# Loads of x four steps later, earlier second halves of W, filling products and earlier copies of R in a fused attention and channel-mix kernel

## The chip, the cores and the metric

The kernel runs on one core of a Trainium2 chip. The core has five engines that run their own instruction queues: TensorE (PE in the profile; its weight loads are PEld), VectorE (DVE), ScalarE (ACT), GpSimd (POOL) and SyncE (SP), which issues nearly all DMAs here. They wait for each other through semaphores. The metric is the device time of one execution in microseconds (us); the time before is 1131.95 us, the median of three runs (1128.4 to 1132.33).

## What is computed

Two layers follow one another. The first is an induced attention: 32 inducing vectors attend over the 12608 rows of x, and the rows of x then attend over the 32 results. The second is a channel mix of width 1024 with a gate, in which every row is mixed with the row before it.

```python
def _attn_ref(x, inducing):              # x: (4, 12608, 128), inducing: (32, 128)
    ...
    def mab(q, kv):
        s = scale * (q @ kv.transpose(0, 2, 1))
        s = s - s.max(-1, keepdims=True)
        a = np.exp(s)
        a /= a.sum(-1, keepdims=True) + 1e-09
        return a @ kv
    h = mab(I, x)
    return mab(x, h).astype(np.float32)

def _moe_ref(x, mu_k, mu_r, w_k, w_v, w_r):   # w_k: (128, 1024), w_v: (1024, 128), w_r: (128, 128)
    x_prev = np.concatenate([np.zeros((B, 1, D), dtype=np.float32), x[:, :-1, :]], axis=1)
    xk = mu_k * x + (1.0 - mu_k) * x_prev
    xr = mu_r * x + (1.0 - mu_r) * x_prev
    k = np.maximum(xk @ w_k, 0.0)
    v = k * k @ w_v
    r = 1.0 / (1.0 + np.exp(-(xr @ w_r)))
    return (r * v).astype(np.float32)
```

All is float32; the kernel splits several float32 matrices into a high part and a low rest (`kh` and `kl`, `ah` and `al`, `wvh` and `wvl`), whose products are added.

## The kernel before

Each of the four batches has 12608 rows: six blocks of 2048 rows and a tail of 320. A block has four groups of 512 rows, so a batch has 25 groups. A group is worked in four **units** of 256 of the 1024 channels, 100 units a batch, 400 in all. The main loop takes one unit in each **step**, and everything else is hung onto these steps by hand: `at(n, f)` runs `f` at the end of step n, `soon(n, f)` runs it in step n right after the unit's first products. Inside an engine the order of the program is the order of execution.

A step n does the following. `up` (L809 and L811) multiplies the attention weights `R` of the group, once as they stand and once shifted by one row, by `W[0]` and `W[1]`, which hold the two mixes of the attention result with w_k (512 columns in the first half, 512 in the second, and 128 for the gate); it writes one of two PSUM tiles `ps_a`. `square` then makes `k_t` on DVE (L821), `kh` on ACT (L826) or, for the steps listed in `high_vector`, on DVE (L823), and the full square on ACT (L827); POOL makes the rest `kl` (L829). `down` (L840, six products) works on the unit of four steps before (`LAG`). In every fourth step `zgate` (L798 and L799) makes the gate, `gate` (L845) and `store` (L856, then the DMAs of L864, one for two groups) the output.

For the next batch, `stage_a` runs beside these units, one block in twelve steps (a **segment**, starting at step s; six beside each of the first three batches, numbered 1 to 18 below): `load_x` (L193) brings a block of x, 1 MB, into one of three buffers `xb`; `btr(c)` for c = 0 to 3, at s-1, s, s+1 and s+3, transposes a quarter of it on DVE (L344) into one of four `xs`, and sends it by four DMAs (L347) to `xt`; `scores` at s+9 (L372, eight products in the profile) multiplies `xt` by the inducing vectors. At step s+1 `load_x` is called for the block that the next segment transposes from its own s-1, which is this segment's s+11. In the same segments `stage_b` turns the block's scores into weights: `low` writes the last of them (L660), and `spread` (L670, four DMAs a group, with the one-column copy `halo`, L593) brings them to `R`; the first of these DMAs that needs `low` waits for it at the head of SP's queue. So SP's queue holds, in the order of the program, the DMAs of `btr`, the loads of x, the spreads and the stores.

The first batch starts differently. `head()` does its first attention, and `start()` orders what stands between it and the first units: `wa` and `wb` are the first and the second halves of `W[0]` and `W[1]`, each as a product (L537), a high part on ACT (L540) and a low rest on DVE (L543); `wg` are the gate's columns. The first four groups of weights do not go by DMA: `place(k)` makes `hi` (ACT, L762), `lo` (DVE, L765) and `put` (transposes on PE, L771, and a copy to `R` on ACT, L773). `spin(n)` makes n products of the identity whose result nobody reads.

The lines that the change touches are L480 and L482 (the loads), L914 to L918 (`spin`), L1013 to L1034 (`start`) and L1037 (`high_vector`).

Of the kernel before, what the change touches and what calls it, by code (L numbers as in the profile page):

```python
# [8 lines left out]
F32 = mybir.dt.float32  # L9
# [10 lines left out]
def kernel(  # L20
# [15 lines left out]
    P = 128  # L36
    Q = 4
    FC = F // P
    G = 512
# [19 lines left out]
    pa = ctx.enter_context(tc.tile_pool(name="pa", bufs=2, space=bass.MemoryType.PSUM))  # L59
# [4 lines left out]
    def pb_tile(bank=None):  # L64

        return pb.tile([P, G], F32, name="pb_" + (bank or next(banks)))
# [92 lines left out]
    def groups(j):  # L159

        w = G if j < NBLK - 1 else TAIL // Q
        return [(j * BLK + i * w, w) for i in range(Q)]
# [16 lines left out]
    def load_x(b, j, pair=None, pieces=1):  # L179

        S = batches[b]
        gr = groups(j)
        w = gr[0][1]
        if w < G:
            t = xn_pool.tile([P, Q, C], F32, name="xl", bufs=1)
            nc.sync.dma_start(out=t[:w], in_=x[b, gr[0][0]:, :].rearrange("(i p) c -> p i c", p=w))
            for i in range(Q):
                S.xn[j, i] = t[:, i:i + 1, :]
            return
        src = x[b, j * BLK:(j + 1) * BLK, :].rearrange("(p s) c -> p s c", p=P)  # L190
        if b > 0:
            t = xn_pool.tile([P, Q * Q, C], F32, name="xb", bufs=3)
            nc.sync.dma_start(out=t, in_=src)  # L193
            S.xb[j] = t
            return
        if pair is not None:
            S.xh[j] = [next(pair).rearrange("p u (k c) -> p (u k) c", c=C) for _ in range(2)]
        else:
            t = xn_pool.tile([P, Q * Q, C], F32, name="xb", bufs=3)
            S.xh[j] = [t[:, :2 * Q, :], t[:, 2 * Q:, :]]  # L200
        n = 2 * Q // pieces
        for h in range(2):
            for o in range(0, 2 * Q, n):
                nc.sync.dma_start(out=S.xh[j][h][:, o:o + n, :], in_=src[:, 2 * Q * h + o:2 * Q * h + o + n, :])
# [121 lines left out]
    def stage_a(b, j, at, t):  # L326
# [8 lines left out]
        jt = NBLK - 1  # L335
# [141 lines left out]
        k = order_a.index((b, j))  # L477
        for bn, jn in order_a[k + 1:]:
            if jn < NBLK - 1:
                at(t + 1, lambda: load_x(bn, jn))  # L480
                if jn == NBLK - 2:
                    at(t + 1, lambda: load_x(bn, jt))  # L482
                break


# [102 lines left out]
    def halo(S, g, far=True):  # L588

        if g == 0:  # L590
            nc.vector.memset(S.R[g].bitcast(F32)[:, 0:1], 0.0)
        elif far:
            nc.sync.dma_start(out=S.R[g].bitcast(F32)[:, 0:1], in_=S.R[g - 1].bitcast(F32)[:, G:G + 1])  # L593
        else:
            nc.vector.tensor_copy(out=S.R[g][:, 0:1], in_=S.R[g - 1].bitcast(F32)[:, G:G + 1])
# [272 lines left out]
    def run(th):  # L868
        for f in th:
            f()  # L870
# [40 lines left out]
    ab = [stage_a_head(j, k, hs) for k, (j, hs) in enumerate(order_h)]  # L911
    weights, hfin, gates, wpart = combine(0)

    def spin(n):  # L914

        ps = pa.tile([P, 2, G], F32, name="ps_a")
        for i in range(n):
            nc.tensor.matmul(out=ps[:, 0, :P], lhsT=ident, rhs=ident, start=True, stop=True)  # L918


    def head():
# [37 lines left out]
        u.sums()  # L959
        v.expo()  # L960
        spin(3)
        w.scores()
        for h in range(2):
# [5 lines left out]
        for c in range(FC // cg):  # L969
            split_wv(c)  # L970
        spin(5)
        v.etrans()
        v.sums()
        v.hmm(0)
        w.etrans()
        w.sums()
        v.acc()
        spin(1)
        weights()
        w.hmm(1)  # L980
# [8 lines left out]
    def at(n, f):  # L989
        events.setdefault(n, []).append(f)  # L990

    def soon(n, f):
        early.setdefault(n, []).append(f)

    def start():

        part0, pl0 = stage_b_head([0, 1])
        part1, pl1 = stage_b_head([2, 3])
        sc0, tu0, df0, ex0, nm0 = part0([0])
        sc1, tu1, df1, ex1, nm1 = part0([1])  # L1000
        sc2, tu2, df2, ex2, nm2 = part1([0, 1])
        (hi0, lo0, put0), (hi1, lo1, put1) = pl0
        box = {}

        def bank():
            return pv.tile([P, G], F32, name="ps_v")

        def gate_bank(s):
            if s == 0:
                box["g"] = bank()  # L1010
            return box["g"][:, s * C:(s + 1) * C]

        wa = [wpart(s, 0, bank) for s in range(2)]  # L1013
        wb = [wpart(s, 1, bank) for s in range(2)]
        wg = [wpart(s, None, lambda s=s: gate_bank(s)) for s in range(2)]
        assert F // G == 2
        S = batches[0]
        run([gates, sc0, sc1, tu0, df0, ex0, wa[0][0], wa[1][0], tu1, nm0, wa[0][1], hi0, wa[1][1], lo0, wa[0][2], put0,
             df1, ex1, wa[1][2], nm1, hi1, lambda: halo(S, 1, far=False)])
        for n, f in ((0, wb[0][0]), (0, wb[0][1]), (1, wb[1][0]), (1, wb[1][1]), (1, put1)):  # L1020
            soon(n, f)
        for n, f in ((0, lo1), (0, wb[0][2]), (1, wb[1][2]), (1, sc2), (2, tu2), (2, df2), (2, ex2), (3, nm2)):
            at(n, f)
        for prod, high, low in wg:
            at(1, prod)
        for prod, high, low in wg:
            at(1, high)
            at(2, low)
        for k, (high, low, put) in enumerate(pl1):
            at(3, high)  # L1030
            at(4, low)
            at(2 * k + 6, put)
            at(4 * k + 4, lambda k=k: halo(S, k + 2, far=False))
        soon(4, lambda: units[0][0].zgate(first=True))  # L1034

    SEG = 12
    high_vector = {3}  # L1037
    for b in range(B):
        t = b * UB + (4 if b == 0 else 0)
        for j in range(NBLK - 1):  # L1040
            s = t + SEG * j
            high_vector |= {s + 4, s + 8}
            if b + 1 < B:
                stage_a(b + 1, j, at, s)
            first = b == 0 and j == 0
            stage_b(b, j + 1, at, s + 1 + first, first)
        if b + 1 < B:
            s = t + SEG * (NBLK - 1)
            combine(b + 1, at, s)
            stage_b(b + 1, 0, at, s + 13, b == 0)  # L1050
# [6 lines left out]
    with tc.manual_schedule():  # L1057
        head()
        start()
        for n in range(len(units) + LAG + 2):  # L1060
            grp, u = units[n] if n < len(units) else (None, n % NU)
            old, ou = units[n - LAG] if LAG <= n < len(units) + LAG else (None, 0)
            m = n - LAG - 1
            if 0 <= m < len(units) and units[m][1] == NU - 1:
                units[m][0].gate()
            if grp is not None:
                grp.up(u)
                run(early.pop(n, []))
                if n >= NU and u == 1:
                    grp.zgate()  # L1070
                low = grp.square(u, n in high_vector)
                low(nc.vector if n == end else nc.gpsimd, 0, grp.w)
            if 1 <= m <= len(units) and units[m - 1][1] == NU - 1:
                units[m - 1][0].store()
            if old is not None:
                old.down(ou)
            run(events.pop(n, []))
# [30 lines left out]
```

## Time and profile before

| what | before |
|---|---|
| median of three runs | 1131.95 us (1128.4 to 1132.33) |
| profiled execution, time | 1130.93 us |
| profiled execution, span | 1128.7 us |
| PE busy | 1098.4 us (97%) |
| ACT, POOL, DVE busy | 969.8, 952.9, 912.0 us |
| PE busy from 0 to 44 us | 35.14 of 44 us |
| PE busy from 44 to 75 us | 24.74 of 31 us |
| PE busy from 75 to 320 us | 243.92 of 245 us |
| PE busy from 320 to 600 us | 274.81 of 280 us |
| PE busy from 600 to 850 us | 247.63 of 250 us |
| PE busy from 850 us to the end | 272.19 of 278.7 us |

The profile is of one execution on the chip. Matmuls overlap in the records (each of the up products is listed with 0.40 us, and the next starts 0.23 us later), and their ends are modelled, so a wait of PE shows as a gap or as a group of products that takes longer than its equals. In the rows of the order of time, the columns are the start and the length in us, the engine (SPq is SP's queue at the issue of a DMA), the line, the operation, what is written and read, and the count; brackets give the idle time before and what ended it. The granted clock of PE is a column of its own in the table of windows (PEclk).

### The profile page before, as it was taken

How to read it: one execution, taken by the hardware profiler on the slowest of the kernel's cores; microseconds unless marked ns; L12 is line 12 of the kernel's file. 1: busy time of each engine (PE TensorE's matmuls, PEld its weight loads, DVE VectorE, ACT ScalarE, POOL GpSimd, SP SyncE). 2: the span in 40 equal slices, each digit the busy share in tenths (PEclk: the TensorE clock that was granted, in tenths of full speed). 3: DMA queues.
4: the chain of work that ended last, by engine and by line, in shares of the span. 5: the costliest groups of instructions: out<-in, count | busy, mean ns of one | idle time of the engine just before them, and what ended most of it. 6: DMA issues, size and time to landing. Idle time of an engine off the chain costs nothing.

```text
span 1128.7 us, 17615 instructions
## 1 busy us (share of the span) xinstructions
PE 1098.4 (97%) x5699; PEld 834.1 (74%) x5699; DVE 912.0 (81%) x1318; ACT 969.8 (86%) x1096; POOL 952.9 (84%) x417
## 2 busy tenths in 40 slices
PE   7889999999999999999999999999999999999997
PEld 5567777777776777777777777777778777777886
DVE  6798889887787999887777889898777888887665
ACT  6588888888888888887998889888889999989996
POOL 2279888888897888898888988888888899999997
PEclk9999999999999999999999999999999999999999
DMA  9024555642334655554144554654223233242212
GB/s 344 4 77 89 112 126 119 139 122 36 60 75 109 133 124 117 118 103 104 23 81 88 111 123 113 134 133 82 50 52 62 44 63 61 56 76 57 44 29 34
DMA packets 264458, 102.30 MB, mean 91 GB/s; under 512 B 234256, under 2 KB 237488, under 8 KB 262064
## 3 DMA queue, kind: packets, MB, share of 16 engines
q1 hardware_dynamic: 263360, 101.10, 41.0%
q8 instruction: 45, 0.74, 0.3%
q14 instruction: 45, 0.37, 0.1%
q10 hardware_dynamic: 1008, 0.10, 0.1%
HBM read 28.07 MB, written 25.82 MB: 48 GB/s over the span
## 4 chain that ended last, share of the span: by engine, by line
PE 78%; DVE 9%; ACT 5%; DMA 3%; issue 3%; SPq 1%; POOL 1%; DVEq 0%; ACTq 0%; POOLq 0%
PE ps_v L840 39%; PE ps_a L809 15%; PE ps_a L811 14%; DVE k_t L821 3%; PE pb_a L372 2%; PE pb_b L616 2%; ACT kh L826 2%; PE ps_v L798 2%; PE ps_v L799 2%; DMA xt<-xs 2%; PE pb_a L441 1%; ACT k_t L827 1%; SPq L347 1%; DMA xb<-in_x_dram 1%; POOL kl L829 1%
## 5 line engine op out<-in xcount | busy, mean ns | idle before, releaser
L829 POOL TENSOR_TENSOR kl<-k_t,kh 128x1024 fp32r<-128x1024 f32 (+1 forms) x399 | 938.5, 2385 | 140.7 <-ACT k_t L827 106.7
L821 DVE TENSOR_SCALAR k_t<-ps_a 128x1024 f32<-128x1024 f32 (+1 forms) x400 | 479.6, 1199 | 146.8 <-PE ps_a L811 123.2
L827 ACT ACTIVATE k_t<-k_t 128x1024 f32<-128x1024 f32 (+1 forms) x400 | 418.4, 1048 | 37.6 <-DVE kh L823 25.6
L826 ACT ACTIVATE kh<-k_t 128x1024 fp32r<-128x1024 f32 (+1 forms) x351 | 364.8, 1039 | 85.2 <-PE ps_v L840 49.5
L809 PE MATMUL ps_a<-R,W 128*128 128x512 f32 (+1 forms) x800 | 324.6, 406 | 4.1 <-ACT R L773 2.8
L811 PE MATMUL ps_a<-R,W 128*128 128x512 f32 (+1 forms) x800 | 314.6, 393 | 0.2 <-DVE W L543 0.2
L840 PE MATMUL ps_v<-kh,wvh 128*128 128x512 f32 (+1 forms) x800 | 247.8, 391 | 0.0
L840 PE MATMUL ps_v<-kl,wvh 128*128 128x512 f32 (+1 forms) x800 | 246.7, 390 | 0.7
L840 PE MATMUL ps_v<-kh,wvl 128*128 128x512 f32 (+1 forms) x800 | 247.0, 390 | 0.0
L809 PEld LDWEIGHTS ps_a<-R,W 128*128 128x128 f32 x800 | 151.2, 189 | 78.0 <-issue 14.4
L840 PEld LDWEIGHTS ps_v<-kl,wvh 128*128 128x128 f32 x800 | 148.5, 188 | 37.6 <-POOL kl L829 5.3
L840 PEld LDWEIGHTS ps_v<-kh,wvh 128*128 128x128 f32 x800 | 149.5, 188 | 34.7
L840 PEld LDWEIGHTS ps_v<-kh,wvl 128*128 128x128 f32 x800 | 149.5, 188 | 33.8
L811 PEld LDWEIGHTS ps_a<-R,W 128*128 128x128 f32 x800 | 150.9, 189 | 31.4 <-DVE W L543 0.8
L845 DVE TENSOR_TENSOR oT<-ps_v,rT 128x512 f32<-128x512 f32 (+1 forms) x100 | 66.6, 666 | 1.8
L856 DVE STREAM_TRANSPOSE ot<-oT 128x512 f32<-128x512 f32 x96 | 67.1, 699 | 0.0
L823 DVE SCALAR_TENSOR_TENSOR kh<-ps_a,k_t 128x1024 fp32r<-128x1024 f32 x49 | 60.0, 1224 | 5.1
L801 ACT ACTIVATE rT<-ps_v 128x512 f32<-128x512 f32 (+1 forms) x99 | 57.8, 584 | 0.3
L344 DVE STREAM_TRANSPOSE xs<-xb 128x512 f32<-128x512 f32 x72 | 49.9, 693 | 0.2
L801 ACT ACT_TABLE_LOAD x31 | 39.8, 1283 | 0.6
L798 PE MATMUL ps_v<-R,W 128*128 128x512 f32 (+1 forms) x99 | 39.0, 394 | 0.4 <-DVE oT L845 0.4
L799 PE MATMUL ps_v<-R,W 128*128 128x512 f32 (+1 forms) x99 | 38.7, 391 | 0.0
(211 smaller groups left out, 618.2 us busy)
## 6 DMA issues: line engine op xcount, KB each, us to landing
out_dram<-ot SPq DMA_DIRECT2D x184, 128.0 KB, 3.3
xb<-in_x_dram SPq DMA_DIRECT2D x18, 1024.0 KB, 6.1
xt<-xs SPq DMA_DIRECT2D x288, 64.0 KB, 2.0
R<-ah SPq DMA_DIRECT2D x184, 64.0 KB, 2.0
R<-al SPq DMA_DIRECT2D x184, 64.0 KB, 2.0
kl<-in_x_dram SPq DMA_DIRECT2D x4, 512.0 KB, 9.5
xb<-in_x_dram SPq DMA_DIRECT2D x4, 512.0 KB, 10.8
W<-ah SPq DMA_DIRECT2D x24, 64.0 KB, 2.0
```

What stands on the lines that cost most here:

```text
L798: nc.tensor.matmul(out=ps[:, :w], lhsT=S.W[0][:, F:WF], rhs=R[:, 1:w + 1], start=True, stop=False)
L799: nc.tensor.matmul(out=ps[:, :w], lhsT=S.W[1][:, F:WF], rhs=R[:, 0:w], start=False, stop=True)
L801: nc.scalar.activation(out=self.rT, in_=ps[:, :w], func=AF.Sigmoid)
L809: nc.tensor.matmul(out=ps[:, c, :w], lhsT=S.W[0][:, cs], rhs=R[:, 1:w + 1], start=True, stop=False)
L811: nc.tensor.matmul(out=ps[:, c, :w], lhsT=S.W[1][:, cs], rhs=R[:, 0:w], start=False, stop=True)
L821: nc.vector.tensor_scalar(out=k, in0=self.ps[:, :, :w], scalar1=0.0, scalar2=None, op0=ALU.max)
L826: nc.scalar.activation(out=kh, in_=k, func=AF.Square)
L827: nc.scalar.activation(out=k, in_=k, func=AF.Square)
L829: return lambda eng, a, z: eng.tensor_tensor(out=kl[:, :, a:z], in0=k[:, :, a:z], in1=kh.bitcast(F32)[:, :, a:z], op=ALU.subtract)
L840: nc.tensor.matmul(out=self.v, lhsT=wt[:, fc, :], rhs=kk[:, c, :], start=(fc == 0 and n == 0), stop=(fc == FC - 1 and n == 2))
L845: nc.vector.tensor_tensor(out=self.oT, in0=self.v, in1=self.rT, op=ALU.mult)
L856: nc.vector.transpose(out=ot[:, o:o + w], in_=self.oT)
```

## The change

```diff
@@ stage_a
         k = order_a.index((b, j))
         for bn, jn in order_a[k + 1:]:
             if jn < NBLK - 1:
-                at(t + 1, lambda: load_x(bn, jn))
+                at(t + 5, lambda: load_x(bn, jn))
                 if jn == NBLK - 2:
-                    at(t + 1, lambda: load_x(bn, jt))
+                    at(t + 5, lambda: load_x(bn, jt))
                 break
@@ spin
-    def spin(n):
+    def spin(n, ps=None):
 
-        ps = pa.tile([P, 2, G], F32, name="ps_a")
+        ps = ps or pa.tile([P, 2, G], F32, name="ps_a")
@@ start
+        def first_bank():
+            return pb_tile("a")
+
...
-        wb = [wpart(s, 1, bank) for s in range(2)]
+        wb = [wpart(s, 1, (first_bank, bank)[s]) for s in range(2)]
...
-        run([gates, sc0, sc1, tu0, df0, ex0, wa[0][0], wa[1][0], tu1, nm0, wa[0][1], hi0, wa[1][1], lo0, wa[0][2], put0,
+        run([gates, sc0, sc1, tu0, df0, ex0, wa[0][0], wa[1][0], wb[0][0], lambda: spin(2), tu1, nm0, wa[0][1], hi0,
+             wa[1][1], wb[0][1], lo0, wa[0][2], put0, lambda: spin(2),
              df1, ex1, wa[1][2], nm1, hi1, lambda: halo(S, 1, far=False)])
-        for n, f in ((0, wb[0][0]), (0, wb[0][1]), (1, wb[1][0]), (1, wb[1][1]), (1, put1)):
+        for n, f in ((0, wb[1][0]), (0, wb[1][1]), (2, put1)):
             soon(n, f)
-        for n, f in ((0, lo1), (0, wb[0][2]), (1, wb[1][2]), (1, sc2), (2, tu2), (2, df2), (2, ex2), (3, nm2)):
+        for n, f in ((0, wb[0][2]), (0, lo1), (0, wb[1][2]), (1, sc2), (2, tu2), (2, df2), (2, ex2), (3, nm2)):
             at(n, f)
...
-            at(2 * k + 6, put)
+            soon(2 * k + 6, put)
...
-    high_vector = {3}
+    high_vector = set()
```

The loads of x for a coming segment are asked for at step s+5 instead of s+1. In `start`, the second half of `W[0]` is multiplied before the first transposes of weights, into the bank `pb_a`, and the second half of `W[1]` in step 0 instead of step 1; two products of the identity stand before and two behind the first transposes; the second group's transposes and copy to R come in step 2 instead of 1, the third's and fourth's at the front of steps 6 and 8 instead of the end; and the square of step 3 is made on ACT instead of DVE.

On SP, in segment 3, from the DMAs of the third quarter of a block of x (`xt<-xs`) to the store behind those of the last quarter, the program before has these rows. `R<-ah` and `R<-al` are a spread, `R<-R` its one-column copy, `xb<-in_x_dram` the load of the next block, `out_dram<-ot` a store.

```order
L347 DMA xt<-xs 32x512 x4
L193 DMA xb<-in_x_dram 128x2048
L593 DMA R<-R 128x1
L670 DMA R<-ah 32x512
L670 DMA R<-al 32x512
L670 DMA R<-ah 32x512
L670 DMA R<-al 32x512
L347 DMA xt<-xs 32x512 x4
L864 DMA out_dram<-ot 32x32x32 x4
```

The changed program has these rows at the same place.

```order
L347 DMA xt<-xs 32x512 x4
L593 DMA R<-R 128x1
L670 DMA R<-ah 32x512
L670 DMA R<-al 32x512
L670 DMA R<-ah 32x512
L670 DMA R<-al 32x512
L347 DMA xt<-xs 32x512 x4
L193 DMA xb<-in_x_dram 128x2048
L864 DMA out_dram<-ot 32x32x32 x4
```

The load has moved from ahead of the spread and the last quarter to behind them. In the segments where a store's step comes earlier it stands behind the store as well; segment 18 has no load in either program.

On PE, around the first unit, the program before has these rows: the first halves of W (`ps_v<-wk_sb`), the first transposes of weights (L771), the first unit, and the second half of `W[0]`.

```order
L537 MATMUL ps_v<-wk_sb,h4k_688 128x512
L537 MATMUL ps_v<-wk_sb,h4k_690 128x512
L771 MATMUL ps_a<-ident,ah 128x128 x4
L809 MATMUL ps_a<-R,W_692 128x512
L811 MATMUL ps_a<-R,W_693 128x512
L809 MATMUL ps_a<-R,W_692 128x512
L811 MATMUL ps_a<-R,W_693 128x512
L537 MATMUL ps_v<-wk_sb,h4k_688 128x512
```

The changed program has these rows there.

```order
L537 MATMUL ps_v<-wk_sb,h4k_688 128x512
L537 MATMUL ps_v<-wk_sb,h4k_690 128x512
L537 MATMUL pb_a<-wk_sb,h4k_688 128x512
L918 MATMUL ps_a<-ident 128x128 x2
L771 MATMUL ps_a<-ident,ah 128x128 x4
L918 MATMUL ps_a<-ident 128x128 x2
L809 MATMUL ps_a<-R,W_692 128x512
L811 MATMUL ps_a<-R,W_693 128x512
L809 MATMUL ps_a<-R,W_692 128x512
L811 MATMUL ps_a<-R,W_693 128x512
L537 MATMUL ps_v<-wk_sb,h4k_690 128x512
```

The second half of `W[0]` and two fillers stand ahead of the transposes, two fillers behind them, and the second half of `W[1]` takes the place behind unit 0 that the second half of `W[0]` had.

On ACT, around the third group's copy to R (L773), the program before has these rows: the second gate (L801), the squares of units 5 and 6, and the copy.

```order
L801 ACTIVATE rT<-ps_v 128x512
L826 ACTIVATE kh<-k_t 128x1024
L827 ACTIVATE k_t<-k_t 128x1024
L826 ACTIVATE kh<-k_t 128x1024
L827 ACTIVATE k_t<-k_t 128x1024
L773 CAST R<-pb_a 128x512
```

The changed program has these rows there.

```order
L801 ACTIVATE rT<-ps_v 128x512
L826 ACTIVATE kh<-k_t 128x1024
L827 ACTIVATE k_t<-k_t 128x1024
L773 CAST R<-pb_a 128x512
L826 ACTIVATE kh<-k_t 128x1024
L827 ACTIVATE k_t<-k_t 128x1024
```

The copy has moved ahead of one unit's two squares.

## The prediction

> **What bounds the kernel now.** I read the chain that ended last on the page first, then that chain in order of time, then what the engines did around each wait of PE on it.
>
> ```profile
> PE 78%; DVE 9%; ACT 5%; DMA 3%; issue 3%; SPq 1%; POOL 1%; DVEq 0%; ACTq 0%; POOLq 0%
> ```
>
> PE carries the end, so a pause of PE is time lost unless something else is late as well. DMA holds 3% of the chain. Followed in order of time, those pieces end at one line: the scores of the next batch (L372), which read `xt`. These are the eighteen segments' scores where PE lost time there, and first one where it lost none (segment 17):
>
> ```profile
> 759.79 1.06 PE L372 MATMUL pb_a<-xt,indT 128*32 128x512 f32 x8
> ...
> 154.34 1.59 PE L372 MATMUL pb_a<-xt,indT 128*32 128x512 f32 x8
> ...
> 221.17 1.85 PE L372 MATMUL pb_a<-xt,indT 128*32 128x512 f32 x8 [0.71 <-DVE ot L856]
> ...
> 351.06 2.63 PE L372 MATMUL pb_a<-xt,indT 128*32 128x512 f32 x8 [2.69 <-DMA xb<-in_x_dram]
> ...
> 385.96 2.10 PE L372 MATMUL pb_a<-xt,indT 128*32 128x512 f32 x8
> ...
> 453.62 1.98 PE L372 MATMUL pb_a<-xt,indT 128*32 128x512 f32 x8 [1.00 <-DMA xt<-xs]
> ...
> 520.94 1.93 PE L372 MATMUL pb_a<-xt,indT 128*32 128x512 f32 x8 [1.05 <-DMA xt<-xs]
> ...
> 625.25 1.70 PE L372 MATMUL pb_a<-xt,indT 128*32 128x512 f32 x8 [0.80 <-DMA xt<-xs]
> ...
> 659.32 1.44 PE L372 MATMUL pb_a<-xt,indT 128*32 128x512 f32 x8 [0.59 <-DMA xt<-xs]
> ...
> 726.23 1.86 PE L372 MATMUL pb_a<-xt,indT 128*32 128x512 f32 x8 [0.79 <-DMA xt<-xs]
> ...
> 792.30 2.15 PE L372 MATMUL pb_a<-xt,indT 128*32 128x512 f32 x8
> ```
>
> Undisturbed, the eight products take 1.06 us. Each row's loss is its length over 1.06 plus the idle time in brackets: 0.53 (segment 3), 1.50 (5), 4.26 (7), 1.04 (8), 1.92 (10), 1.92 (12), 1.44 (13), 0.97 (14), 1.59 (16), 1.09 (18). That the loss is not made up later shows in the chain, where the scores of the other stage (L616) mark equal places of three segments:
>
> ```profile
> 398.00 1.00 PE pb_b L616 x8
> ...
> 430.69 0.99 PE pb_b L616 x8
> ...
> 465.58 0.99 PE pb_b L616 x8
> ```
>
> 32.69 us without a loss, 34.89 with the 1.92 of segment 10. The transfers are late because SP is late. Segment 10's last quarter was transposed by DVE some 13 us before its DMAs were issued:
>
> ```profile
> 436.55 0.70 DVE L344 STREAM_TRANSPOSE xs<-xb 128x512 f32<-128x512 f32 x1
> ...
> 446.27 0.53 SPq L193 DMA_DIRECT2D xb<-in_x_dram  x1
> 446.91 0.52 SPq L593 DMA_DIRECT2D R<-R  x1
> ...
> 450.07 2.96 SPq L347 DMA_DIRECT2D xt<-xs  x4
> 453.15 2.93 SPq L864 DMA_DIRECT2D out_dram<-ot  x4
> ...
> SPq L347 <- DMA xb<-in_x_dram: 11.3, 13, 1.2
> ```
>
> SP issues one DMA after another; the load takes 0.64 us of this queue (446.27 to 446.91), its megabyte stands ahead of the quarter's bytes, and 13 times an `xt` DMA waited at issue for the load to land (the last row, from the waits of SP).
>
> **The loads (L480, L482).** No instruction is added or removed; the load moves behind the last quarter's four DMAs. What the quarter does without a load ahead of it is in the trace: segment 18 has none. These are the issues of the last quarter there and in the two others that I need:
>
> ```profile
> 789.48 2.43 SPq L347 DMA_DIRECT2D xt<-xs  x4
> ...
> 517.29 3.07 SPq L347 DMA_DIRECT2D xt<-xs  x4
> ...
> 722.36 3.24 SPq L347 DMA_DIRECT2D xt<-xs  x4
> ```
>
> In segment 18 the scores end 792.30 + 2.15 - 789.48 = 4.97 us after the first issue; in segments 10, 12 and 16 it was 5.53, 5.58 and 5.73. With the load away, the first issue comes 0.64 us earlier and the scores can end 4.97 behind it: 1.20, 1.25 and 1.40 us earlier, leaving 0.7, 0.7 and 0.2 of their losses. The same sum gives more than the loss in segments 3, 5, 7, 8, 13 and 14, so theirs go whole: 0.53 + 1.50 + 4.26 + 1.04 + 1.44 + 0.97 = 9.74. Segment 18 keeps its 1.09. Together 9.74 + 1.20 + 1.25 + 1.40 = **13.6 us**. Segment 7's pause also cost clock:
>
> ```profile
> 352.00:354.00 2.00, 2.00 (x8) 0.38 (x2) 0.27 (x1) 1.06 (x1) 2.00 (x2) 0.50 0.18 33
> 354.00:356.00 2.00, 2.00 (x8) 1.60 (x8) 0.98 (x2) 0.00 (x0) 2.00 (x2) 0.81 0.00 0
> ```
>
> The scores were over at 353.69, but the granted clock (third number from the end) was at half until about 354.8 (0.81 is the mean of the second window); 1.1 us at half speed are **0.5 us** more.
>
> What the load is moved past: the spread's five DMAs and the quarter's four, all earlier now, and in every second segment a store's four (2.93 us to issue). What it must meet is the next segment's first transpose on DVE (L344), where `k_t` of the units would queue behind it.
>
> ```profile
> 460.92 0.71 DVE L344 STREAM_TRANSPOSE xs<-xb 128x512 f32<-128x512 f32 x1
> ...
> DMA to landing us min/median/max: 5.5/6.1/11.8
> ```
>
> For segment 10: quarter issued from 449.43, done in about 2.4 us as in segment 18, load from 451.8, landed at the median of 6.1 us by 457.9; the transpose, 1.20 earlier than before, comes at 459.7. 1.8 us are to spare. I take 0 for it; the bounds are 0 and what the third rival gives. Behind the load the store's bytes come later; the next that SP waits for is `al` at the first spread, and that hides it.
>
> **The start (L1013 to L1037).** PE waits there for R and W, in turn:
>
> ```profile
> 46.09 0.66 PE L771 MATMUL ps_a<-ident,ah 128*128 128x128 f32 x4 [1.81 <-DVE ah L765]
> 47.42 0.69 PE L809 MATMUL ps_a<-R,W 128*128 128x512 f32 x1 [0.68 <-ACT R L773]
> ...
> 49.00:50.00 1.00, 1.00 (x3) 0.55 (x2) 0.45 (x1) 0.29 (x1) 0.00 (x0) 0.50 0.00 0
> ...
> 48.79 0.15 DVE L595 CAST R<-R 128x1 fp32r<-128x1 f32 x1
> ...
> 49.55 1.22 DVE L821 TENSOR_SCALAR k_t<-ps_a 128x1024 f32<-128x1024 f32 x1 [0.61 <-PE ps_a L811]
> ...
> 51.82 0.69 DVE L543 TENSOR_TENSOR W<-ps_v,W 64x512 fp32r<-64x512 f32 x1 [0.71 <-ACT W L540]
> ...
> 57.47 0.47 PE L809 MATMUL ps_a<-R,W 128*128 128x512 f32 x1 [0.46 <-DVE k_t L821]
> ...
> 58.44 1.06 ACT L827 ACTIVATE k_t<-k_t 128x1024 f32<-128x1024 f32 x1
> ...
> 59.41 0.40 ACT L737 ACTIVATE s<-s 128x256 f32<-128x256 f32 x1
> ...
> 64.19 1.28 ACT L801 ACT_TABLE_LOAD   x1
> ...
> 72.58 0.57 ACT L773 CAST R<-pb_a 128x512 fp32r<-128x512 f32 x1
> 73.21 0.49 PE L809 MATMUL ps_a<-R,W 128*128 128x512 f32 x1 [2.09 <-ACT R L773]
> ```
>
> The product of `W[0]`'s second half and the fillers go into the pause of 1.81 us and the one of 0.68 us: no time of their own, and unit 0 still starts at 47.42. PE then works at half clock, from about 47.6 to 51.0 by the windows, of which one is quoted; I take it that filled pauses keep the clock. Then unit 0 is done by 48.6 and DVE, free at 48.9, starts L821 there instead of at 49.55, until 50.2. Behind it stand the two low parts of W (about 0.6 each) and `lo1` (0.4), until 51.9; unit 1's L821 until 53.1, unit 2's until 54.3. Unit 2 has its W by then. ACT makes units 0 and 1 (four squares of 1.05), the gate's W (0.4) and the second group's R, which is there at about 56.1; unit 4 starts then, instead of at 57.47. From there ACT's queue is the bound up to the third group's R: L737 0.4, squares of units 2 to 5, eight of 1.05, two casts of weights 0.75, the table load 1.25, two gates 1.2, the copy 0.57: 12.6 us, so 68.7 instead of 73.15. PE's own work in that stretch is some 11.7 us (four units with their downs at 2.3, two gates, L616 and the transposes) and fits. Unit 8 thus starts near 68.7 instead of 73.21. Of these 4.5 us 2.1 come from the copy passing one unit's squares; the square of unit 3, moved to ACT, costs 1.05 and frees 1.22 on DVE, both counted. ACT is left with less slack behind unit 8, where its next squares come only some 2.4 us earlier than before while PE comes 4.5 earlier; the down of unit 9 has 0.8 to spare by my count. I take **4.3 us**, bounds 0 and 4.6.
>
> A rule of the Trainium skill, "TensorE: Matmul & The Clock Gate", Part 1 on the clock gate, speaks against the fillers: the clock falls after an idle window of about 3.4 us, and no pause here is that long. By it the half clock at 47.6 has another cause and would stay, and the sum would be the 1113.1 us worked out below. The trace shows 0.50 right behind pauses of 1.81 and 0.68 us, and again behind 2.69 us in segment 7, and I go by the trace.
>
> The sum: 13.6 + 0.5 + 4.3 = 18.4 us off the profiled execution (1130.93, of which the span is 1128.7), which lies 1.0 below the median of the runs: **1112.5 us**.
>
> **The rivals.** *SP stays late without the load.* For it: segment 18 has no load and loses 1.09. If each segment kept up to that much, only 0.41 + 3.17 + 0.83 + 0.83 + 0.35 + 0.50 = 6.1 would go, with 0.5 and 4.3: 1120.0. Against it: the first issues are earlier by the load's own 0.64, and the quarters' issues took 2.96 to 3.24 us with the load ahead against 2.43.
>
> *The start gives nothing.* ACT, not PE, is the bound from unit 8 on, and the units' squares take back what R gained: 1116.8. If the clock falls at 47.6 all the same, unit 1 and all behind it come 0.6 us later: 1113.1.
>
> *The load comes too late for the next transposes.* Fifteen loads are followed by a segment of the same batch. From 6.1 + 1.8 = 7.9 us to landing on, DVE stands at L344. PE can go on for one unit of 2.3 us at most, as `ps_a` has two tiles. At the longest landing seen, 11.8 us, DVE stands 3.9 us and PE loses 1.6 to 3.9; at 2.8 over fifteen segments 42 us are lost against 18.4 won: 1154.5, **slower**. From about 1.6 us a segment on (10 us to landing) it is slower by more than 0.5%. A mild case, half of the loads late by 1 us, gives 1120.0. Against it: the long landings were at the head of the program, where loads of x and of weights stood in line.
>
> **How the numbers follow.** Forecast 0.58; the clock falls all the same 0.12; SP stays late 0.08; the start gives nothing 0.10; loads mildly late 0.08; loads late throughout 0.04. The range goes from 1108, where the residues of segments 10, 12 and 16 and the start's 0.3 go too and the execution is a fast one, to 1121, which holds the rivals at 1116.8 and 1120.0. About 0.5% (5.7 us) is what a measurement here tells from no change. All but the last case are faster by more: 0.94 faster, 0.02 within, 0.04 slower.
>
> **What would show it.** In the changed profile the L372 groups take 1.06 us in segments 3, 5, 7, 8, 13 and 14, and still about 1.1 more in segment 18; the wait of SP's L347 for the load is gone from the table; L616 to L616 is below 33 us throughout batch 1. The granted clock is 1.00 from 47 to 51 us, unit 8 starts near 69, and L344 waits for no load. I am wrong if DVE's wait for `xb` appears at L344, if L372 still waits as in segment 18 everywhere, or if PE pauses between units 8 and 16.

## The result, and the profile after

| | before | changed |
|---|---|---|
| median of five runs beside each other | 1131.95 us (1127.04 to 1132.41) | 1115.65 us (1113.84 to 1117.51) |
| ratio, 95% interval | 1 | 0.9868 (0.9846 to 0.9891) |
| profiled execution, time and span | 1130.93, 1128.7 us | 1117.51, 1115.1 us |
| PE busy from 320 to 600 us, from 600 to 850 us | 274.81, 247.63 us | 278.08, 249.80 us |

The change takes 16.3 us off the median; 18.4 off the profiled execution were forecast. The median lies 3.2 above the forecast 1112.5. The changed execution that was profiled is the slowest of its five (the spans of the others are 1111.6 to 1113.4 us), so the two profiles differ by 13.4 us only.

The shares of the chain that ended last, in the changed kernel:

```profile
PE 86%; DVE 5%; ACT 4%; DMA 3%; issue 1%; POOL 1%; SPq 0%; ACTq 0%; DVEq 0%; POOLq 0%
```

PE now holds 86% of the chain, where it held 78%, and DVE 5% instead of 9%: fewer detours. The scores (L372) of the same segments as before, from PE's rows in order of time; segments 1 and 18 are the ends of what is called the middle below:

```profile
84.05 1.06 PE L372 MATMUL pb_a<-xt,indT 128*32 128x512 f32 x8
...
149.73 1.50 PE L372 MATMUL pb_a<-xt,indT 128*32 128x512 f32 x8
...
215.68 1.83 PE L372 MATMUL pb_a<-xt,indT 128*32 128x512 f32 x8
...
342.77 1.07 PE L372 MATMUL pb_a<-xt,indT 128*32 128x512 f32 x8
...
375.60 2.00 PE L372 MATMUL pb_a<-xt,indT 128*32 128x512 f32 x8
...
442.10 1.46 PE L372 MATMUL pb_a<-xt,indT 128*32 128x512 f32 x8
...
509.80 2.62 PE L372 MATMUL pb_a<-xt,indT 128*32 128x512 f32 x8 [0.32 <-PE ps_v L840]
...
614.36 1.06 PE L372 MATMUL pb_a<-xt,indT 128*32 128x512 f32 x8
...
647.10 1.68 PE L372 MATMUL pb_a<-xt,indT 128*32 128x512 f32 x8
...
713.39 1.06 PE L372 MATMUL pb_a<-xt,indT 128*32 128x512 f32 x8
...
778.66 2.18 PE L372 MATMUL pb_a<-xt,indT 128*32 128x512 f32 x8
```

No group waits for `xt` with PE standing idle any more, and segments 7, 13 and 16 lose nothing. But segments 3, 5, 8, 10, 12 and 14 still take 0.44, 0.77, 0.94, 0.40, 1.88 and 0.62 us too long (length over 1.06, with the bracket), 5.05 in sum, where those up to segment 17 lost 15.17 before. Segment 18, which has no load, lost 1.09 and loses 1.12. The scores of the other stage (L616) in the chain say the same for batch 1:

```profile
387.54 1.00 PE pb_b L616 x8
420.23 0.99 PE pb_b L616 x8
453.55 0.99 PE pb_b L616 x8
487.88 0.30 PE pb_b L616 x8
```

32.69, 33.32 and 34.33 us, where the forecast had under 33 throughout. What is new is on DVE, in its rows of the transposes that read `xb`:

```profile
190.47 0.71 DVE L344 STREAM_TRANSPOSE xs<-xb 128x512 f32<-128x512 f32 x1 [1.05 <-DMA xb<-in_x_dram]
...
484.43 0.71 DVE L344 STREAM_TRANSPOSE xs<-xb 128x512 f32<-128x512 f32 x1 [2.33 <-DMA xb<-in_x_dram]
...
753.56 0.71 DVE L344 STREAM_TRANSPOSE xs<-xb 128x512 f32<-128x512 f32 x1 [0.92 <-DMA xb<-in_x_dram]
```

Three times DVE now waits for the load itself. Behind each wait comes a segment whose scores are late (5, 12 and 18), and the largest also stops PE outright, through the product with the gate (L845) that queues behind the transpose on DVE:

```profile
485.77 0.50 PE L798 MATMUL ps_v<-R,W 128*128 128x512 f32 x1 [1.27 <-DVE oT L845]
```

At the start the clock (PEclk, third number from the end in the windows) is whole where it was half:

```profile
48.00:49.00 1.00, 1.00 (x5) 0.62 (x4) 1.00 (x1) 0.56 (x2) 0.00 (x0) 1.00 0.00 0
49.00:50.00 1.00, 0.57 (x3) 0.13 (x1) 0.94 (x3) 1.00 (x2) 0.00 (x0) 1.00 0.00 0
```

**Where the time went.** For this and all runs below, each profile is cut at three of PE's rows that every version has: the last product of the head (L517), the scores of segment 1 and those of segment 18. Before: 40.86, 88.66, 792.30, end 1128.7. Changed: 39.80, 84.05, 778.66, end 1115.1. The head, which the change doesn't touch, was 1.06 us shorter in this execution; the start (L517 to segment 1) went from 47.80 to 44.25, 3.55 less; the middle (segment 1 to 18) from 703.64 to 694.61, 9.03 less; the rest stayed (336.40, 336.44). With 0.18 more outside the span, that is the 13.4.

### The profile page after: what moved, and what is told of

Its sections match the earlier page's. It is cut to its first block, busy times and chain, and to the rows that moved or that the text cites. A ratio compares the mean times of both kernels' runs of the same rounds, so it can differ in the third digit from the quotient of the medians.

```text
span 1115.1 us, 17659 instructions
## 1 busy us (share of the span) xinstructions
PE 1093.0 (98%) x5707; PEld 830.1 (74%) x5707; DVE 911.3 (82%) x1317; ACT 969.8 (87%) x1097; POOL 953.0 (85%) x417
## 4 chain that ended last, share of the span: by engine, by line
PE 86%; DVE 5%; ACT 4%; DMA 3%; issue 1%; POOL 1%; SPq 0%; ACTq 0%; DVEq 0%; POOLq 0%
PE ps_v L840 44%; PE ps_a L809 16%; PE ps_a L811 15%; PE pb_b L616 2%; PE pb_a L372 2%; PE ps_v L798 2%; PE ps_v L799 2%; DVE k_t L821 2%; DMA xb<-in_x_dram 2%; PE pb_a L441 2%; ACT kh L826 1%; ACT k_t L827 1%; DMA kl<-in_x_dram 1%; POOL kl L829 1%; DMA mur<-in_moe_mu_r_dram 0%
## 5 line engine op out<-in xcount | busy, mean ns | idle before, releaser
L845 DVE TENSOR_TENSOR oT<-ps_v,rT 128x512 f32<-128x512 f32 (+1 forms) x100 | 66.7, 667 | 1.8
L801 ACT ACTIVATE rT<-ps_v 128x512 f32<-128x512 f32 (+1 forms) x99 | 57.9, 585 | 0.3
L344 DVE STREAM_TRANSPOSE xs<-xb 128x512 f32<-128x512 f32 x72 | 50.0, 694 | 4.9 <-DMA xb<-in_x_dram 4.3
L798 PE MATMUL ps_v<-R,W 128*128 128x512 f32 (+1 forms) x99 | 39.1, 395 | 1.6 <-DVE oT L845 1.6
```

The costliest lines, as they stand in the source:

```text
L798: nc.tensor.matmul(out=ps[:, :w], lhsT=S.W[0][:, F:WF], rhs=R[:, 1:w + 1], start=True, stop=False)
L801: nc.scalar.activation(out=self.rT, in_=ps[:, :w], func=AF.Sigmoid)
L845: nc.vector.tensor_tensor(out=self.oT, in0=self.v, in1=self.rT, op=ALU.mult)
```

## The experiments

All runs in one table, each in five rounds beside the kernel before, whose median there was 1129.93 to 1131.95 us; runs of different rows are compared by their ratios. "Waits" is what DVE's L344 waited for `xb`, in sum and times. "Old" and "new" are the starts before and after the change, "step" is where the loads of x are asked for.

| run | median us | ratio to before, 95% | start | middle | waits |
|---|---|---|---|---|---|
| before (old, step 1) | 1131.95 | 1 | 47.80 | 703.64 | none |
| changed (new, step 5) | 1115.65 | 0.9868 (0.9846 to 0.9891) | 44.25 | 694.61 | 4.3, 3 |
| e11, changed again | 1116.86 | 0.9877 (0.9860 to 0.9895) | 44.24 | 692.53 | 2.9, 2 |
| e1, old, step 5 | 1117.96 | 0.9889 (0.9869 to 0.9909) | 49.22 | 692.74 | 5.3, 2 |
| e2, new, step 1 | 1125.48 | 0.9955 (0.9938 to 0.9972) | 44.27 | 704.85 | none |
| e4, new, step 4 | 1112.56 | 0.9836 (0.9817 to 0.9854) | 44.26 | 688.50 | none |
| e13, e4 again | 1111.18 | 0.9837 (0.9810 to 0.9863) | 44.25 | 688.30 | none |
| e9, old, step 4 | 1116.29 | 0.9885 (0.9867 to 0.9904) | 49.22 | 688.68 | none |
| e6, new, step 9 | 1152.20 | 1.0193 (1.0170 to 1.0216) | 44.27 | 726.27 | 35.1, 9 |
| e5, new, step 1 on ACT | 1182.21 | 1.0467 (1.0442 to 1.0492) | 44.28 | 763.57 | none |
| e3, changed, no fillers | 1119.44 | 0.9895 (0.9877 to 0.9913) | 44.93 | 694.60 | 4.1, 3 |
| e7, changed, copies back | 1116.88 | 0.9895 (0.9876 to 0.9914) | 47.46 | 691.99 | 3.7, 2 |
| e10, e4 and small DMAs | 1119.29 | 0.9901 (0.9883 to 0.9918) | 44.30 | 693.52 | none |
| e12, e4, halos on DVE | 1109.67 | 0.9817 (0.9794 to 0.9841) | 44.22 | 688.26 | none |

**Which half gives what.** The change split in two. e1 is the kernel before with

```diff
-                at(t + 1, lambda: load_x(bn, jn))
+                at(t + 5, lambda: load_x(bn, jn))
```

(and the same for the tail's load); e2 is the changed kernel with the opposite edit.

> Kernel before, with the loads of x at step 5 of each segment and the old start. Theory (the loads carry most): L372 falls late by 15.2 us in the ten segments of the kernel before and by 5.0 us in those of the changed kernel, so 10 us less than before (9 to 11.5); the prediction on record had 13.6 us for this part. The rows of L372 stand as in the changed kernel (waits for xb at L344 in the segments whose load stands behind a store), and the clock of 48 to 51 us is 0.50 again. Rival (the start carries most): 6 us less than before or under.

> Changed kernel, with the loads of x back at step 1 of each segment; the new start is kept. Theory: the start is worth what L372 of segment 1 shows without the earlier head, 3.6 us (3 to 5) less than before, and the losses at L372 of segments 5, 7, 8, 10, 12, 13 are those of the kernel before (1.5, 4.3, 1.0, 1.9, 1.9, 1.4 us). Together with the loads alone it makes the sum of both, 14 to 17 us. Rival (the two overlap: an earlier start brings SP's queue no earlier, so that its gain is lost at the next late quarter): under 1.5 us less than before.

The loads alone took 13.1 us off the median (1131.01 beside them), more than was expected, and 10.90 off the middle; the start alone took 5.5 off the median and 3.53 off its own stretch, with the middle's losses back (704.85). So both halves are real, and neither rival holds. Their sum, 18.6, is more than the 14 to 17 expected, and more than the 16.3 that the whole change took off. The start of e1 took 1.4 us longer than that of the kernel before, though its code is the same; that is taken up at the clock.

**Why the middle keeps losses.** Against the changed kernel, e4 only has `t + 4` in place of `t + 5`. On SP this changes the order in nine places: there the load goes ahead of the store's four DMAs, as it does in the other segments already. e6 has `t + 9`, so that the load stands behind a store everywhere.

> Changed kernel, with the loads of x at step 4 instead of 5, so that in every segment they stand ahead of the store on SP. Theory (what is left of the loss comes from the load that stands behind a store, takes 5.7 us more to land and holds L344 back): L344's waits for xb (1.05, 2.33 and 0.92 us) are gone, L372 of segments 5 and 12 loses under 0.4 us instead of 0.8 and 1.9, and the time is 1.5 to 2.7 us under the changed kernel. Rival (single issues of SP that take 1.8 us instead of 0.6 make the loss, wherever they fall): within 0.7 us of the changed kernel, with late L372 at other segments. Second rival (four stores behind a load take 4.2 to 5.8 us to issue instead of 3.0 and make R's copies late): 1 us over the changed kernel or more.

> Changed kernel, with the loads of x at step 9 instead of 5, so that they stand behind a store on SP in every segment, where the changed kernel has that in every second one. Theory (a load that stands behind a store's 2.9 us of issues misses the next segment's L344 by 1 us or so): waits of L344 for xb in most segments, 8 us or more in sum against 4.3, L372 from segment 1 to 18 takes 3 to 8 us more than the 694.6 us of the changed kernel, and the time is 1118.5 to 1124. Rival (the place of the load against the store does not matter): L372 from segment 1 to 18 within 1.5 us of 694.6, and the time within 1.5 us of 1115.7.

e4 took 18.5 us off the median where the changed kernel took 16.3 and, the second time, 14.3 off. DVE waits for no load, the middle is 15.14 us shorter than before instead of 9.03, and e13 repeats it (688.30). The place where the largest wait was, on SP, in the changed kernel (segment 11; the four DMAs of the last quarter, the store, the loads):

```profile
470.39 2.43 SPq L347 DMA_DIRECT2D xt<-xs  x4
...
472.92 3.03 SPq L864 DMA_DIRECT2D out_dram<-ot  x4
476.05 0.82 SPq L193 DMA_DIRECT2D xb<-in_x_dram  x1
```

And in e4, with the transpose that reads what was loaded:

```profile
468.96 2.44 SPq L347 DMA_DIRECT2D xt<-xs  x4
471.49 0.53 SPq L193 DMA_DIRECT2D xb<-in_x_dram  x1
...
472.61 5.53 SPq L864 DMA_DIRECT2D out_dram<-ot  x4
...
481.39 0.71 DVE L344 STREAM_TRANSPOSE xs<-xb 128x512 f32<-128x512 f32 x1
```

From the quarter's first issue the load is issued 5.66 us later with the store ahead, 2.53 without, and the chain has it on its way for 8.35 us (476.05 to 484.40), which is just when the transpose at 484.43 could start. The store behind the load takes 5.53 us to issue instead of 3.03, but the time falls all the same, and by more than was expected: both rivals of e4 fall.

In e6 the effect was far larger than expected: the middle 31.7 us longer than the changed kernel's, where 3 to 8 were expected. In segment 3, the last quarter, the store and the load on SP, and the transpose on DVE that waits for the load, with the product of PE behind it:

```profile
153.45 2.43 SPq L347 DMA_DIRECT2D xt<-xs  x4
158.57 2.71 SPq L864 DMA_DIRECT2D out_dram<-ot  x4
161.37 1.76 SPq L193 DMA_DIRECT2D xb<-in_x_dram  x1
```

```profile
168.99 0.71 DVE L344 STREAM_TRANSPOSE xs<-xb 128x512 f32<-128x512 f32 x1 [4.56 <-DMA xb<-in_x_dram]
...
170.34 0.80 PE L798 MATMUL ps_v<-R,W 128*128 128x512 f32 x1 [3.24 <-DVE oT L845]
```

From the quarter's first issue the load is issued 7.92 us later, where in the changed kernel it was 2.53 (146.28 to 148.81). The store that it was put behind can't be issued before its rows are computed, and SP goes in order: SP issues nothing for 2.69 us (155.88 to 158.57), and the store and the load follow. So the load paid for the store's own wait and not for its issue alone. My size left that out. Seven such waits of 4.4 to 6.3 us stand in DVE's rows. (Three of the waits in the sum are listed under `R<-al`, which had long landed; by the load's median of 7.2 us to landing it was the load.)

What of that reached PE shows in the windows of the middle, in e6 and then in the changed kernel (the stretch, its length, PE's busy time and matmuls, the other engines', and PEclk third from the end):

```profile
84.30:810.57 726.27, 699.94 (x3599) 525.01 (x3599) 593.82 (x843) 609.51 (x680) 604.86 (x257) 0.98 0.47 102
...
84.05:778.66 694.61, 691.89 (x3599) 520.30 (x3599) 593.73 (x843) 609.51 (x680) 605.52 (x257) 1.00 0.49 105
```

PE stood idle for 26.3 us instead of 2.7, of which 25.3 are seven pauses of 3.0 to 4.9 us at L798. The other 8.1 us are longer busy time for the same 3599 matmuls: behind five of the seven pauses the clock was at half for 3.4 or 6.8 us, 27.3 in sum. So a quarter or more of the 31.7 us came by the clock, which the expectation had not counted either.

**Issue or bytes?** Two tries. e5 issues the loads at step 1 on ACT (`eng=nc.scalar` passed to `load_x`), so that SP has none. e10 is e4 with a DMA of 0.5 KB at the load's old place:

```diff
             if jn < NBLK - 1:
+                at(t + 1, lambda: small(bn, jn))
                 at(t + 4, lambda: load_x(bn, jn))
...
+    def small(b, j):
+        p = sm.tile([P, 1], F32, name="small", bufs=2)
+        nc.sync.dma_start(out=p, in_=x[b, j * BLK:j * BLK + P, 0:1])
```

> Changed kernel, with the loads of x back at step 1 but issued by ACT instead of SP. SP's sequence then has no load at all, and its 0.64 us of issue is gone; the megabyte travels ahead of the last quarters, as in the kernel before. Theory A (what made the last quarters late was the load's place on SP: its issue and the xt DMAs that waited there for it): L372 from segment 1 to 18 takes 690 us or less, no wait of L344 for xb, 1113 us or less. Theory B (it was the bytes of the load on the DMA engines): the losses of the run with the start alone return, L372 from segment 1 to 18 near 704.9 us, and the time near 1125. ACT takes 0.6 us for each of the 17 loads, and may stand where its load waits for an earlier transfer: up to 10 us more if all of it were on PE's path.

> The run with the new start and the loads at step 4, with one added DMA of 0.5 KB (one column of x, used by nothing) on SP at step 1 of each segment that has a load, where the load stood in the kernel before. It takes SP's time without the megabyte. Theory A (what the load cost there was its issue, since the last quarter comes as late as SP is): L372 from segment 1 to 18 takes 5 us or more over the 688.5 of the run without it, a third or more of the 15.1 us that the place is worth, and the time is 1116 or more. Theory B (the cost was the megabyte: its bytes ahead of the quarter's, and SP's DMAs that waited for it to land): 2.5 us or less over, since 0.6 us of issue fits into what SP has to spare, and the time is under 1115.

e5 answered neither: it is 52.3 us slower than the kernel before, far outside both theories. In its waits of SP stand new rows:

```profile
SPq L670 <- DMA xb<-in_x_dram: 63.0, 9, 8.6
...
SPq L593 <- DMA xb<-in_x_dram: 24.3, 3, 8.1
```

SP has no load to issue and yet waits for ACT's loads to land: in the trace the program's 1145 DMAs share eight semaphores in rotation (143 or 144 each), and each waits at issue for the one eight earlier, whoever issues it. While such a wait lasts the spreads and quarters behind it stand. The Trainium skill, "Trainium Kernel Development and Optimization", section on key constraints, says that issuing from several engines saves the issue time only. Here it cost far more than it saved: against e2, the same but for the queue, the middle is 58.7 us longer. PE stood for 29.1 of them and was busy for 29.6 longer, in part at half clock (0.97 in the mean of the middle, 1.00 in e2). Which is the dearer, the bytes or the issue, stayed open here.

e10 tells what a DMA costs there that moves hardly any bytes. Its issues on SP (shortest, median and longest in ns):

```profile
L208 SPq DMA_DIRECT2D small<-in_x_dram x17: 580/580/1084, 65.6 to 735.8; - x17
```

Who waited for the quarters' transfers, and how long in sum (L376 is L372 there, as the added function moves the lines by four):

```profile
who waited for it (us, times):
  PEld pb_a L376: 2.7, 6
```

Seventeen DMAs of 0.58 us and hardly any bytes make the middle 5.0 us longer than e4's (693.52 against 688.50), the weight loads of the scores wait 2.7 us for them instead of 0.5, and by the ratios the time is some 7 us more. So of the 15.1 us that the load's place is worth, a third comes with a DMA there that moves next to nothing. I read that as SP's time; the small DMA also takes a place in the rotation of semaphores, which was not tried apart. The other 10 are what the megabyte adds, its bytes ahead of the quarter's or the DMAs that wait for it to land. Those two weren't told apart.

If SP's time counts so much, taking some of it away should help. e12 moves 52 of SP's 93 one-column copies (L593) to DVE, five steps after the spread; those of the first three blocks of each batch stay, since their columns are needed sooner. e13 is e4 again, beside it.

```diff
-                halo(S, j * Q + i)
+                if j < 3:
+                    halo(S, j * Q + i)
...
             at(t + 10 + i, lambda i=i: spread(i))
+            if j >= 3 and (full or i == 0):
+                at(t + 15 + i, lambda i=i: halo(S, j * Q + i, far=False))
```

> The run with the new start and the loads at step 4, with 52 of SP's 93 one-column copies of R (L593, 0.5 to 1.5 us of SP each) made by DVE instead, five steps after the spread, when the column has landed (0.15 us each on DVE). Segments 7, 8, 9, 13 and 14 keep some of SP's. Theory (SP's issue time is what sets the last quarter's lateness): what is left of the losses at L372 (0.3 to 0.4 us in segments 10, 12, 14 and 18, 1.6 in sum) goes to under 0.5, and the time is 0.5 to 2 us under the run without it. Rival (the rest is no longer SP's): the losses stay and DVE's copies cost up to 1 us.

> The run with the new start and the loads at step 4 again, unaltered, beside the one with the copies on DVE. 1111.5 to 1113.5 us, L372 from segment 1 to 18 688 to 689.5 us, no wait of L344 for xb. If the first run was a good draw: 1114 or more, or waits for xb.

The median is 1.5 us lower than e13's, but the intervals of the ratios overlap widely, and the middle is the same (688.26, 688.30): not told apart. So it is not shown that SP's time still holds the middle back in e4; the theory of e12 failed. e12 and e4 are both faster than the changed kernel and the kernel before.

**The residues.** e11 is the changed kernel a second time.

> The changed kernel itself, unaltered, since the execution that was profiled was the slowest of its five. Theory (the losses that are left at segments 5 and 12 come from L344's wait for xb, those at 3, 8 and 14 from single long issues on SP that fall elsewhere in another execution): waits for xb at L344 of 3.5 to 5 us in sum, before segments 5, 12 and 18 again, losses at 5 and 12 again, those at 3, 8 and 14 moved or gone; L372 from segment 1 to 18 693 to 695 us. Rival (all of them are fixed by the program): the same segments lose the same, within 0.2 us.

The scores of segments 10 and 12 and the waits ahead of them, on PE and DVE:

```profile
440.55 2.16 PE L372 MATMUL pb_a<-xt,indT 128*32 128x512 f32 x8
...
508.24 2.62 PE L372 MATMUL pb_a<-xt,indT 128*32 128x512 f32 x8
```

```profile
415.03 0.71 DVE L344 STREAM_TRANSPOSE xs<-xb 128x512 f32<-128x512 f32 x1 [0.84 <-DMA xb<-in_x_dram]
...
483.26 0.71 DVE L344 STREAM_TRANSPOSE xs<-xb 128x512 f32<-128x512 f32 x1 [2.04 <-DMA xb<-in_x_dram]
```

The wait ahead of segment 12 is there again with its loss; those ahead of segments 5 and 18 are gone, which lose 0.01 and 0.63 now, and one ahead of segment 10 has come, with 1.10. Expected were all three at the same places. So a wait brings a loss, in each of the twelve waits of this and the other runs at step 5, but which segments have one is partly chance. A loss can also come without a wait: e10 has none and loses 2.17 in segment 12. Segments 3 and 14 lost nothing this time and segment 8 lost 0.50. That single long issues on SP make these was not shown. In segment 3 the long issue is in the second quarter, and it is there both times (four DMAs in 3.31 us, 3.66 the first time, where 2.43 is usual). The last quarter was issued in 2.43 us in both, and the scores ended 4.95 us behind its first issue in both; it came 0.31 us earlier this time, with PE 0.11 later, and the loss went from 0.44 to 0.03. What makes a single issue last 1.2 us or more was not found.

**The start.** e3 is the changed kernel without its four fillers; e7 has the copies to R (`put1`, and `put` of the third and fourth group) and step 3's square back where they were:

```diff
-        for n, f in ((0, wb[1][0]), (0, wb[1][1]), (2, put1)):
+        for n, f in ((0, wb[1][0]), (0, wb[1][1]), (1, put1)):
...
-            soon(2 * k + 6, put)
+            at(2 * k + 6, put)
...
-    high_vector = set()
+    high_vector = {3}
```

> Changed kernel without the two pairs of filling products at the start. Theory (pauses without work take the clock down): granted clock of 0.50 for about 3 us near 50 us, as before, 0.6 to 1.7 us more than the changed kernel. Rival (these pauses are too short to cost the clock, or the products that come earlier fill them): clock 1.00, within 0.5 us of the changed kernel.

> Changed kernel, with the second group's copy to R back in step 1, the third's and fourth's back at the end of steps 6 and 8, and step 3's square back on DVE; the earlier W and the filling products stay. Theory (the copies' place makes unit 8 wait, W and the clock give the rest): from L517 to L372 of segment 1 46 to 47 us instead of 44.3, a pause of about 2 us ahead of unit 8, and 1.5 to 3 us over the changed kernel. Rival (ACT's squares bound that stretch whatever the copies' place): 44.3 to 45 us there, and the time within 0.7 us of the changed kernel.

Without the fillers PE's pauses ahead of the transposes and of unit 0 are open (rows of PE), and the clock is half for some 3 us (one window):

```profile
46.55 0.66 PE L771 MATMUL ps_a<-ident,ah 128*128 128x128 f32 x4 [0.95 <-DVE ah L765]
47.88 0.50 PE L809 MATMUL ps_a<-R,W 128*128 128x512 f32 x1 [0.68 <-ACT R L773]
...
49.00:50.00 1.00, 1.00 (x4) 0.81 (x3) 0.36 (x3) 0.37 (x1) 0.00 (x0) 0.50 0.00 0
```

The start takes 0.68 us more, where 0.6 was forecast. By the ratios the time is 2 to 3 us over the changed kernel's, with intervals that overlap; the head, which has the same code, was 1.5 us longer in this profile, and the middle is the same, so I read the fillers as worth 0.7. With the copies back, PE stands again ahead of unit 8, and the clock falls behind that pause:

```profile
71.48 0.77 PE L809 MATMUL ps_a<-R,W 128*128 128x512 f32 x1 [2.09 <-ACT R L773]
...
73.00:74.00 1.00, 1.00 (x4) 0.81 (x3) 0.36 (x1) 0.98 (x2) 1.00 (x2) 0.50 0.91 156
```

47.46 us, 3.2 more than the changed kernel: with the fall of the clock that comes with it, the copies' place is nearly all of the start's gain. By the ratios it is 2 to 3 us over the changed kernel, as expected, again with intervals that overlap.

Do start and loads add up? e9 is the kernel before with the loads at step 4.

> Kernel before, with the loads of x at step 4 and the old start. Theory (start and loads add up, and step 4 is worth 15.1 us between L372 of segment 1 and of segment 18): 688.5 us there (687.5 to 690), 47.8 to 49.2 us from L517 to L372 of segment 1, and 3.5 to 5.5 us over the run with the new start and step 4, so 1116 to 1118. Rival (the good run with step 4 was a lucky place of SP's long issues): 692 us or more between the two L372, and over 1119.5.

At step 4 they do: the middle is 688.68, the start 49.22, and by the ratios the time is 5.5 us over e4's, where the starts differ by 4.96. The middle does not depend on the start.

## Why the prediction was right, and where not

**The bound.** Right. The late quarters stood on SP behind the load: with its place back at step 1 the middle is 704.85 (e2), with step 4 688.5. SP's wait at L347 for the load, 11.3 us in sum before, is gone from the waits of the changed kernel, as forecast.

**The loads, 13.6 us and 0.5 of clock.** The mechanism was right and the term too large: 9.03 and 11.1 us in two executions of the changed kernel. The step that failed is the one behind "1.8 us are to spare". It was worked out for segment 10, where the load stands ahead of the store, and the text took 0 for all segments. In every second one the store's four DMAs, whose 2.93 us stood in the same paragraph, come first: 1.8 - 2.9 = -1.1, and the waits found are 0.36 to 2.70 us, in two or three of the nine such segments of an execution; why the others had no wait stays open. So the third rival came true in its mild form, as the forecast named its sign ("DVE's wait for `xb` appears at L344"). The account closes: 15.17 - 5.05 of losses gone, 0.5 of clock, less the 1.27 that PE stood at L798, makes 9.35 against 9.03 measured. With the store behind the load (e4) the term is 15.1, more than forecast, since most of the residues of segments 10, 12 and 16 goes too.

**Single segments.** Segments 7, 13 and 16 went as forecast or better, 10 kept 0.40 of the 0.7, and 18 its 1.09. Segments 3, 5, 8 and 14 were to go whole and kept 0.44 to 0.94; 12 kept 1.88 instead of 0.7, behind the wait of 2.33. "SP stays late without the load" holds for segment 18 alone, and not as a fixed price: with step 4 that segment lost 0.42 and 0.02 (e4, e13), with no load of its own in either kernel, so 1.09 is not what a quarter without a load must lose. SP's time was weighed too low all the same: e10 shows 5.0 us over the segments for a DMA that moves hardly anything.

**The start, 4.3 us.** 3.55 between the two profiles; against the old start with the second fall of the clock (e1, e9) 5.0. Unit 8 started at 67.46 us, 4.8 earlier against unit 0 where 4.5 were forecast, but part was given back behind it, the sign that the forecast named (rows of PE):

```profile
73.38 0.49 PE L809 MATMUL ps_a<-R,W 128*128 128x512 f32 x1 [0.23 <-DVE kh L823]
...
78.78 0.47 PE L809 MATMUL ps_a<-R,W 128*128 128x512 f32 x1 [0.50 <-DVE k_t L821]
```

At these two places PE waits for DVE, not for ACT. Of the parts, the fillers were sized right (0.7 for the clock, 0.6 forecast), and the copies, with the square, are worth 3.2 instead of 2.1, as the clock hangs on them too; less the 1.4 us that its second fall cost in e1 and e9, 1.8 are left by my estimate. The earlier second half of W was not tried by itself.

**The sum.** 18.4 forecast; 16.3 by medians. In the profiles the loads gave 3 to 5 less than the term and the start 0.8 less; the median of the changed kernel lies 1.9 below its execution that was profiled, and that of the kernel before 1.0 above its own.

## What to carry to other kernels

A transfer moved down an in-order queue has to meet its reader in each kind of place that it gets: add up what stands ahead of it there, with what those wait for themselves, and not in one segment that looks typical. A queue that issues one DMA in 0.6 us is a resource like an engine; seventeen needless small DMAs cost 5 us here. Moving DMAs to another engine's queue doesn't free the first if they share a rotation of semaphores.

## What the runs showed of the hardware

The clock fell behind pauses that I had not counted. Ahead of unit 8 the old start pauses for 2.05 to 2.09 us. In the profile of the kernel before it stays whole behind that pause, in those of e1, e7 and e9 it is half for some 3 us; up to there PE's code is the same in e1, e9 and the kernel before. PE's rows of e1 and its window two microseconds on:

```profile
71.90 0.50 PE L809 MATMUL ps_a<-R,W 128*128 128x512 f32 x1 [2.05 <-ACT R L773]
...
74.00:75.00 1.00, 1.00 (x4) 0.75 (x3) 0.89 (x2) 1.00 (x1) 1.00 (x2) 0.50 0.84 156
```

From the last product of the head to unit 8 the three take 32.35, 32.09 and 32.16 us (before, e1, e9), so the 1.4 us by which the start of e1 and e9 (49.22) is longer than that of the kernel before (47.80) come behind that pause. The place of the loads does not move the start (44.27 in e2, 44.25 in the changed kernel), so the clock is the difference that is left. So the same pause costs the clock in one execution and not in another. Its length alone does not decide: in e6 the clock fell behind a pause of 3.24 us and stayed whole behind two of 3.03 and 3.32, and in e3 it fell behind 0.95 and 0.68 us that stand close together. The Trainium skill, "TensorE: Matmul & The Clock Gate", Part 1, has the clock fall after an idle window of about 3.4 us; the runs differ from it in the length of the pause. The new start, whose longest pause is 1.40 us (ahead of unit 4), kept the clock and took 44.22 to 44.30 us in every profile that kept all of it. Of the kernel before, the executions with a mean clock of 0.994 had spans of 1127.6 to 1131.5 us and the two with 0.999 had 1123.5 and 1126.6, so such falls are likely a part of its spread, and of what the change gains.
